# Key blocks transposed three products behind their own, and divisions put first, in a linear-attention and gated-MLP kernel

## The chip, the cores and the metric

The kernel runs on one core of a Trainium2 chip. The time is device microseconds of one execution: the median of three runs before the change is 2389.95 us (2389.79 to 2392.02). One execution was taken with the hardware profiler.

## The reference, cut to what matters

All arrays are fp32: x is 2048 x 1024, there are 32 heads of 32, and the MLP is 3584 wide. The output is the input plus attention times the activated MLP:

```python
xn = layernorm(x)
q, k, v = heads(xn @ wqkv)
phi = lambda t: where(t > 0, t + 1, exp(t)) + 1e-6
kv  = einsum("bhsd,bhse->bhde", phi(k), v)      # 32 x 32 per head
den = einsum("bhqd,bhd->bhq", phi(q), phi(k).sum over s) + 1e-6
s   = (phi(q) @ kv / den) @ wo
g   = silu((silu(xn @ w1) * (xn @ w3)) @ w2)
out = x + s * g
```

## The kernel before, in words

An fp32 product is made of three TensorE matmuls on high and low parts (`mm3`, L103 to L105; `split`, L95 and L96, makes the parts on ScalarE and VectorE). A 2 x 2 block product takes seven such products instead of eight (Strassen-Winograd); they are named by the weight operand, B11, T2, T3, T1, B21, T4, B22, and each is 12 matmuls of 128 x 512. `gemm` runs these seven, and between them VectorE forms the results from the banks a, b, c, d: c22 after T3 and T1, the first quadrant after B21, c21 after T4, c12 after B22 (L457 to L493). A name such as `ck1_0` is bank c of the key product of half 1, pair 0; `wk`, `wq`, `wg`, `wu` are weights of keys, queries, gates and ups.

The rows are taken in two halves of 1024 (h = 0, 1). In order of time the stages are: loading and normalising; keys, then queries of half 0; gates and ups of half 0; keys and queries of half 1, pair 0 of both product by product side by side, the other pairs one after another (757 to 927 us); the row products, which multiply keys and input rows (`g<-xy`, to 1107 us); gates and ups of half 1 (to 1690 us); the attention product (`cs`, `as` and so on with operands XA11s, XS3s, to 1835 us); the second MLP product.

A key block goes through `phi` (two ScalarE steps and a VectorE step, L499 to L501) into a tile `pk`, is then transposed by TensorE in four matmuls into a bank `trk` (`turn`, L507) and stored from there. `pk` has one of four buffers (`signed`), which it shares with the query blocks `pq` and others. `key_rows` puts each transposition into a list `later`. `gemm` calls `catch_up` after each product but the last: this does one transposition from `later` if there is one, and otherwise one step of the first entry of `jobs`, a list of generators that fill the gaps with other work. A job's step may be told (`issue_after`) to come behind a given instruction of its own engine.

In the gates of half 1 the job is `attention_work`: it multiplies g with the value weights (`kv<-gw`, L913), merges wo into it, and divides. `divide(m, k)` loads blocks of phi(q) (`pq_d`) and of the reciprocal denominators (`r_d`) with SyncE (L877, L879; SP in the trace), multiplies them and forms four sums on VectorE (L885, L730 to L734), and stores the operand blocks of the attention product (`qs_d`) through GpSimd's queue. There are 32 divisions, k = 0 to 3 for each m = 0 to 7. The gates and ups of half 1 call `catch_up` 28 x 6 = 168 times; `attention_work` has 152 steps. Its tiles come from four job buffers, which the jobs of the row products use too, and they are loaded some entries ahead of the steps. The attention product reads `qs_d` for m = 0 to 7 in that order.

The scheduler places instructions of an engine in the order that the code and its own estimates give; each engine then runs its instructions in that order.

Of the kernel before, what the change touches and what calls it, by code (L numbers as in the profile page):

```python
# [16 lines left out]
P = 128  # L17
# [5 lines left out]
def tile_linear_attention_times_swiglu(  # L23
# [12 lines left out]
    S, D = x.shape  # L36
    F = w1.shape[1]
    ND = D // P
# [3 lines left out]
    NCH = S // C  # L42
# [362 lines left out]
    def product(acc, B, A, start, stop=True):  # L405
        K = ND // 2
        for k in range(K):
            mm3(acc, (B[:, 0, k], B[:, 1, k]), (A[:, 0, k], A[:, 1, k]),
                start=start and k == 0, stop=stop and k == K - 1)

    later = []
    jobs = []

    def catch_up(*marks):

        if later:
            later.pop(0)()
        elif jobs:
            job, in_order = jobs[0]
            with ExitStack() as behind:  # L420
                for m in marks + (tuple(fetched) if in_order else ()):
                    behind.enter_context(tc.issue_after(m.ins))
                if next(job, None) is None:
                    jobs.pop(0)

    def gemm(B, A, use, early=False, paired=False, own=False):

        name = B.name

        B.upto("B11")
        u = (st.tile([P, C], F32, tag="own", bufs=1, name=f"u{name}") if own else
             pe.tile([P, C], F32, tag="u", name=f"u{name}"))
        ba = bank(f"a{name}")
        product(ba, B.upto("B11"), A["A11"], True)  # L440
        copied = nc.scalar.copy(out=u, in_=ba)
        if early:
            catch_up(copied)
            yield
            product(ba, B.upto("B21"), A["A12"], False)
            use(0, 0, ba)
            yield
            for _ in B.stages:
                pass
        else:  # L450
            next(stages, None)
            catch_up(copied)
            if paired:
                yield
        bb, bc, bd = (bank(f"{n}{name}") for n in "bcd")
        product(bb, B.upto("T2"), A["S2"], True)
        added = nc.vector.tensor_add(out=u, in0=bb, in1=u)  # L457
        next(stages, None)
        catch_up(copied, added)
        if paired:  # L460
            yield
        product(bc, B.upto("T3"), A["S3"], True)
        c22 = small(f"c22{name}")
        added = nc.vector.tensor_add(out=c22, in0=bc, in1=u)
        next(stages, None)
        catch_up(copied, added)
        if paired:
            yield
        product(bd, B.upto("T1"), A["S1"], True)
        added = nc.vector.tensor_add(out=c22, in0=bd, in1=c22)  # L470
        use(1, 1, c22)
        next(stages, None)
        catch_up(copied, added)
        if paired:
            yield
        if not early:
            product(ba, B.upto("B21"), A["A12"], False)
            use(0, 0, ba)
            next(stages, None)
            catch_up(copied, added)  # L480
        if paired:
            yield
        product(bc, B.upto("T4"), A["A22"], False)
        c21 = small(f"c21{name}")
        added = nc.vector.tensor_add(out=c21, in0=bc, in1=u)
        use(0, 1, c21)
        next(stages, None)
        catch_up(copied, added)
        if paired:
            yield  # L490
        product(bd, B.upto("B22"), A["S4"], False)
        c12 = small(f"c12{name}")
        nc.vector.tensor_add(out=c12, in0=bd, in1=u)  # L493
        use(1, 0, c12)
        next(stages, None)
# [17 lines left out]
    def key_rows(h, pair):  # L513

        rows = {}

        def use(n, c, src):
            j = 2 * pair + n
            pk = signed(f"pk{h}_{j}_{c}")
            z = st.tile([P, 1], F32, tag="z", name="z")  # L520
            phi(src, pk, z)
            nc.vector.scalar_tensor_tensor(zacc[:, j:j + 1], z, C * 1e-6, zacc[:, j:j + 1],
                                           op0=ALU.add, op1=ALU.add)
            later.append(lambda: turn(n, c, pk))

        def turn(n, c, pk):
            V = nc.vector
            p_ = turned(pk, f"k{h}_{pair}_{n}{c}")
            if (c, n) == (0, 0):
                y00 = small(f"y00_{h}_{pair}")  # L530
                nc.scalar.activation(y00, p_, AF.Identity, bias=eps)  # L531
                keep_keys(h, pair, "Y00", y00)
            elif (c, n) == (1, 1):
                rows["y01"] = job_tile([P, 2, C], f"y01_{h}_{pair}")
                nc.scalar.copy(out=rows["y01"][:, 1], in_=p_)
            elif (c, n) == (1, 0):
# [12 lines left out]

        return use  # L550

    def row_products():
# [39 lines left out]
        for at, s in enumerate(steps):  # L592
            i, h, t = s
            if at + 2 < len(steps):
                data[steps[at + 2]] = load(*steps[at + 2])
            if at + 1 < len(steps):
                split_[steps[at + 1]] = ready(*steps[at + 1])
            if at + 2 == len(steps):
                ops["g1_0_"].ask()
                stages = in_turn(groups[after_rows:])  # L600
            if at + 1 == len(steps):
                for _ in range(3):
                    next(stages)
            begins, ends = s[1:] == ks[0], s[1:] == ks[-1]
            onto = i in (1, 5)
            if begins and not onto:
                b = {m: bank(f"g{i}_{m}") for m in M}
            for e, (x_, y_) in enumerate(split_.pop(s)):
                for m in M:
                    c = slice(m * P, (m + 1) * P)  # L610
                    last = mm3(b[m], (x_[:, 0, c], x_[:, 1, c]), (y_[:, 0], y_[:, 1]),
                               begins and e == 0 and not onto, ends and e == 1)
                    if ends and e == 1:
                        row_sums(i, m, b[m], u, v)
                with tc.issue_after(last.ins):
                    catch_up()
                yield
            del data[s]

# [247 lines left out]
    def divide(m, k):  # L867
# [12 lines left out]
            return t  # L880

        def steps(t):
            for _ in range(3):
                yield True
            nc.vector.scalar_tensor_tensor(t[:, :2], t[:, :2], 1e-6, t[:, 2:], op0=ALU.add, op1=ALU.mult)  # L885
            for _ in four_sums(t[:, 0], t[:, 1], t[:, 2], t[:, 3], nc.vector):
                pass
            t = t.rearrange("p e (n s) -> p (e n) s", s=P)
            nc.gpsimd.dma_start(out=qs_d[m][:, 0, k], in_=t[:, 0])  # L889
            nc.gpsimd.dma_start(out=qs_d[m][:, 1:, k], in_=t[:, 2:])  # L890
            divided.add((m, k))
            yield True
# [66 lines left out]
        return [Job(lambda e=e: load(e), lambda t, e=e: steps(e, t)) for e in range(2)]  # L959


    LATE = S // (2 * P) - 2

    def late_work():
        yield from go_on([divide(m, k) for m in range(LATE, S // (2 * P)) for k in range(ND // 2)])

    H0, H1 = range(NCH // 2), range(NCH // 2, NCH)

    def all_denominators():
        yield from spread_z()  # L970
        yield from go_on([j for c in range(NCH) for j in denominators(c)])

    def attention_work():
        work = []
        for k in range(ND // 2):
            for e, j in enumerate(merge_wo(k)):
                work += key_values(k + e * (ND // 2)) + [j]
        work += [divide(NT * c + g, k) for c in H0 for g in range(NT) for k in range(ND // 2)]
        work += [divide(m, k) for m in range(NT * H1[0], LATE) for k in range(ND // 2)]
        yield from go_on(work, 3)  # L980


# [19 lines left out]
    stages = in_turn(groups[:after_rows])  # L1002
    for h in range(NH):
        half(h)
    jobs.append((late_work(), True))


    GT = 2 * P
# [261 lines left out]
    acc = []  # L1270
# [35 lines left out]
```

## Time and profile before

| | |
|---|---|
| median of three runs | 2389.95 us (2389.79 to 2392.02) |
| the profiled execution | 2391.7 us, span 2389.9 us |
| busy: TensorE, VectorE, ScalarE, GpSimd | 97%, 74%, 39%, 29% |
| mean granted clock of TensorE | 0.991 |
| DMA | 479.69 MB, 201 GB/s |

In the rows of the trace the first number is the start in microseconds, the second the duration, and square brackets hold how long the engine had stood before the instruction and what ended this. PE is TensorE, DVE VectorE, ACT ScalarE, POOL GpSimd; SP is the engine that issues most loads, SPq its queue, in which the issues follow one another. An engine that is busy for most of the span but stands at a few places can be sped up only at those places. The granted clock of a window is the share of full speed that TensorE had.

### The profile page before, as it was taken

To read this page: it belongs to the slowest core of one execution; us is meant where nothing else is said; L and a number is where in the kernel's file an instruction comes from. 1 tells how busy PE (TensorE), PEld (TensorE's weight loads), DVE (VectorE), ACT (ScalarE), POOL (GpSimd) and SP (SyncE) were. 2 spreads that over 40 slices of the span, in tenths; PEclk is the share of its full clock that TensorE was granted. 3 is DMA by queue.
4 is the path that set the end of the run, shared out by engine and by line. 5 is a ranking of instruction groups with operands and counts; after the bars stand their busy time and mean duration, and the time that the engine had idled before them with its cause. 6 is when DMAs were issued, how large, how long until landed. Compare 5 with 4: busy or idle time off the path is not lost.

```text
span 2389.9 us, 30981 instructions
## 1 busy us (share of the span) xinstructions
PE 2313.4 (97%) x10368; PEld 1895.4 (79%) x10368; DVE 1776.6 (74%) x2822; ACT 925.6 (39%) x1639; POOL 693.4 (29%) x852
## 2 busy tenths in 40 slices
PE   6899999999999899999999999999999999999998
PEld 5788888888887677777888888888777788888876
DVE  8887888887877565566777888887665676767698
ACT  5555343423332444433334232324323543343433
POOL 5210434386774111002243334242321000000033
PEclk9999999999999899999999999999999999999999
DMA  6545555666669435776666556564776665766588
GB/s 232 169 168 176 180 165 175 196 222 207 212 216 363 135 108 179 251 262 222 189 182 191 185 166 196 171 190 149 251 229 197 191 206 159 236 197 188 183 272 264
DMA packets 354015, 479.69 MB, mean 201 GB/s; under 512 B 24144, under 2 KB 262736, under 8 KB 353744
## 3 DMA queue, kind: packets, MB, share of 16 engines
q1 hardware_dynamic: 316608, 359.20, 47.4%
q0 software_dynamic: 37248, 118.52, 14.9%
q8 instruction: 81, 1.33, 0.2%
q14 instruction: 78, 0.64, 0.1%
HBM read 308.81 MB, written 172.49 MB: 201 GB/s over the span
## 4 chain that ended last, share of the span: by engine, by line
PE 42%; issue 9%; DMA 7%; DVE 5%; POOL 3%; ACT 1%; SPq 0%; POOLq 0%; DVEq 0%; ACTq 0%
PE g L103 2%; PE g L104 2%; PE g L105 2%; PE cB L103 1%; PE cB L104 1%; PE dB L104 1%; PE dB L103 1%; PE dB L105 1%; PE cB L105 1%; PE aB L103 1%; PE aB L104 1%; PE aB L105 1%; POOL h_d L751 1%; DMA xy<-y_d 1%; DMA qs_d<-qd 1%
## 5 line engine op out<-in xcount | busy, mean ns | idle before, releaser
L751 POOL DMA_DIRECT2D h_d<-sg x112 | 83.0, 741 | 284.4 <-DVE sg L747 184.3
L1073 POOL DMA_DIRECT2D u_d<-uB x32 | 17.4, 542 | 407.4 <-DVE uB L1056 392.8
L96 DVE TENSOR_TENSOR xy<-xy,xy 128x512 fp32r<-128x512 f32 x112 | 74.8, 704 | 67.5 <-ACT xy L95 67.5
L95 ACT CAST xy<-xy 128x512 fp32r<-128x512 f32 x112 | 65.1, 621 | 103.8 <-PE g L105 66.3
L104 PE MATMUL g<-xy,xy 128*128 128x512 f32 x224 | 87.6, 391 | 0.6 <-DVE xy L96 0.6
L105 PE MATMUL g<-xy,xy 128*128 128x512 f32 x224 | 87.2, 390 | 0.0
L103 PE MATMUL g<-xy,xy 128*128 128x512 f32 x224 | 81.6, 398 | 0.7 <-ACT xy L95 0.7
L511 POOL DMA_DIRECT2D y_d<-y x40 | 28.7, 719 | 138.3 <-ACT y L531 56.3
L1056 DVE TENSOR_TENSOR acc<-cB,acc 128x512 f32<-128x512 f32 x50 | 34.4, 689 | 41.5 <-PE cB L105 41.5
L1056 DVE TENSOR_TENSOR acc<-dB,acc 128x512 f32<-128x512 f32 x56 | 38.6, 689 | 31.6 <-PE dB L105 29.9
L889 POOL DMA_DIRECT2D qs_d<-qd x32 | 18.2, 568 | 150.1 <-DVE qd L885 137.9
L731 POOL TENSOR_TENSOR hs<-hs,sg 128x256 f32<-128x256 f32 x56 | 58.1, 1038 | 0.0
L733 POOL TENSOR_TENSOR hs<-sg 128x256 f32<-128x256 f32 x56 | 55.2, 986 | 0.0
L103 PEld LDWEIGHTS g<-xy,xy 128*128 128x128 f32 x224 | 41.6, 188 | 15.2 <-issue 4.5
L669 POOL DMA_DIRECT2D pq_d<-pq x32 | 17.5, 546 | 124.8 <-DVE pq L501 116.9
L730 POOL TENSOR_TENSOR hs<-sg,sg 128x256 f32<-128x256 f32 x56 | 50.1, 894 | 1.2
L104 PEld LDWEIGHTS g<-xy,xy 128*128 128x128 f32 x224 | 42.0, 188 | 10.2 <-DVE xy L96 1.0
L734 POOL TENSOR_TENSOR hs<-sg,hs 128x256 f32<-128x256 f32 x56 | 49.1, 877 | 1.8
L105 PEld LDWEIGHTS g<-xy,xy 128*128 128x128 f32 x224 | 42.1, 188 | 9.0
L759 POOL DMA_DIRECT2D h_d<-hs x60 | 46.1, 769 | 3.8 <-POOL hs L734 2.7
L766 POOL TENSOR_TENSOR w<-w 128x256 f32<-128x256 f32 x28 | 28.1, 1003 | 62.1 <-DMA w<-in_B_w 62.1
L1187 POOL DMA_DIRECT2D s_d<-s x32 | 17.5, 546 | 88.2 <-DVE s L1056 48.5
(5315 smaller groups left out, 8348.2 us busy)
## 6 DMA issues: line engine op xcount, KB each, us to landing
h_d<-hs POOLq DMA_DIRECT2D x60, 256.0 KB, 3.4
h_d<-sg POOLq DMA_DIRECT2D x56, 256.0 KB, 3.4
w<-in_B_w SPq DMA_DIRECT2D x56, 256.0 KB
wt_d<-w SPq DMA_DIRECT2D x28, 512.0 KB
xy<-x_d SPq DMA_DIRECT2D x28, 512.0 KB
xy<-y_d SPq DMA_DIRECT2D x28, 512.0 KB
h_d<-hs SPq DMA_DIRECT2D x52, 256.0 KB
qs_d<-qd POOLq DMA_DIRECT2D x32, 384.0 KB, 3.4
```

The lines of the kernel that those rows point to most:

```text
L95: nc.scalar.copy(out=hi, in_=src)
L96: return nc.vector.tensor_sub(out=lo, in0=src, in1=hi.bitcast(F32))
L103: nc.tensor.matmul(acc, lhsT=wh, rhs=ah, start=start, stop=False, skip_group_check=True)
L104: nc.tensor.matmul(acc, lhsT=wh, rhs=al, start=False, stop=False, skip_group_check=True)
L105: return nc.tensor.matmul(acc, lhsT=wl, rhs=ah, start=False, stop=stop, skip_group_check=True)
L730: e.tensor_add(out=s1, in0=a21, in1=a22)
L731: e.tensor_sub(out=s2, in0=s1, in1=a11)
L733: e.tensor_sub(out=s3, in0=a11, in1=a21)
L734: e.tensor_sub(out=s4, in0=a12, in1=s2)
L751: nc.gpsimd.dma_start(out=h_d[i][2 * h + c][:, 2 * n:4 * n + 2, k], in_=src)
L759: queue.dma_start(out=h_d[i][2 * h + c][:, 6 + 4 * e:10 + 4 * e, k], in_=o[e].rearrange("p (e s) -> p e s", s=P))
L1056: return V.tensor_add(out=c, in0=src, in1=c)
```

## The change

An entry of `later` carries a countdown of three, which every `catch_up` lowers; while it has not run out, `catch_up` goes on with the jobs. Each product of a gemm returns its last matmul, and the TensorE work of a `catch_up`, a transposition or a job's step, is put behind that matmul. `attention_work` starts with the eight divisions of m = 0 and 1, then has the key-value work, then the divisions of m = 2 to 7. A division takes three steps instead of four, so that the total stays 152. `late_work`, which held the eight divisions of m = 6 and 7 for the attention product, is gone.

```diff
     def product(acc, B, A, start, stop=True):
         for k in range(K):
-            mm3(acc, (B[:, 0, k], B[:, 1, k]), (A[:, 0, k], A[:, 1, k]),
-                start=start and k == 0, stop=stop and k == K - 1)
+            last = mm3(acc, (B[:, 0, k], B[:, 1, k]), (A[:, 0, k], A[:, 1, k]),
+                       start=start and k == 0, stop=stop and k == K - 1)
+        return last
     def catch_up(*marks):
-        if later:
-            later.pop(0)()
+        for e in later:
+            e[0] -= 1
+        if later and later[0][0] <= 0:
+            with ExitStack() as behind:
+                for m in marks[-1:]:
+                    behind.enter_context(tc.issue_after(m.ins))
+                later.pop(0)[1]()
         elif jobs:
...
-        product(bc, B.upto("T3"), A["S3"], True)
+        last = product(bc, B.upto("T3"), A["S3"], True)
         c22 = small(f"c22{name}")
         added = nc.vector.tensor_add(out=c22, in0=bc, in1=u)
         next(stages, None)
-        catch_up(copied, added)
+        catch_up(copied, added, last)
...
-            later.append(lambda: turn(n, c, pk))
+            later.append([3, lambda: turn(n, c, pk)])
...
-                with tc.issue_after(last.ins):
-                    catch_up()
+                catch_up(last)
...
         def steps(t):
-            for _ in range(3):
+            for _ in range(2):
                 yield True
...
-    LATE = S // (2 * P) - 2
-    def late_work():
-        yield from go_on([divide(m, k) for m in range(LATE, S // (2 * P)) for k in range(ND // 2)])
...
     def attention_work():
-        work = []
+        work = [divide(m, k) for m in range(2) for k in range(ND // 2)]
         for k in range(ND // 2):
             for e, j in enumerate(merge_wo(k)):
                 work += key_values(k + e * (ND // 2)) + [j]
-        work += [divide(NT * c + g, k) for c in H0 for g in range(NT) for k in range(ND // 2)]
-        work += [divide(m, k) for m in range(NT * H1[0], LATE) for k in range(ND // 2)]
+        work += [divide(m, k) for m in range(2, S // (2 * P)) for k in range(ND // 2)]
         yield from go_on(work, 3)
...
-    jobs.append((late_work(), True))
```

The first place is the end of pair 0 in half 1. TensorE before, where `dq` is the last product of the pair and `ak1_1` the first of the next:

```order
L105 MATMUL dq1_0__6513<-S4_1_6426,B22q1_0__6562 128x512
L507 MATMUL trk1_0_00_6643<-ident_63,pk1_0_0_6633 128x128 x4
L507 MATMUL trk1_0_01_6694<-ident_63,pk1_0_1_6685 128x128 x4
L103 MATMUL ak1_1__6776<-A11_1_6420,B11k1_1__6588 128x512
L104 MATMUL ak1_1__6776<-A11_1_6420,B11k1_1__6588 128x512
```

TensorE after:

```order
L105 MATMUL ak1_1__6765<-A11_1_6420,B11k1_1__6588 128x512
L513 MATMUL trk1_0_01_6784<-ident_63,pk1_0_1_6677 128x128 x4
L103 MATMUL bk1_1__6795<-S2_1_6421,T2k1_1__6633 128x512
L104 MATMUL bk1_1__6795<-S2_1_6421,T2k1_1__6633 128x512
L103 MATMUL ck1_1__6796<-S3_1_6422,T3k1_1__6611 128x512
```

The block `trk1_0_01` has moved behind the twelve matmuls of `ak1_1`; `trk1_0_00` has moved forward, behind the first two matmuls of `cq1_0` with T4. In pairs 1 to 3, where keys are followed by queries, `trk_00` and `trk_01` stood together ahead of the query product's `aq`; now `aq`, `bq` and `cq` stand ahead of, between and behind them: `aq`, `trk_00`, `bq`, `trk_01`, `cq`, `trk_10`, and between T4 and `trk_01` there are 38 matmuls.

VectorE at the same place before, from the next weights' sums (L346) to the key block `pk1_0_1`:

```order
L346 TENSOR_TENSOR wk1_1__6565<-wk1_1__6565 128x4x128 x2
L96 TENSOR_TENSOR T3k1_1__6618<-wk1_1__6565,T3k1_1__6618 128x512
L346 TENSOR_TENSOR wk1_1__6565<-wk1_1__6565 128x4x128
L485 TENSOR_TENSOR c21k1_0__6683<-ck1_0__6492,uk1_0__6455 128x512
L485 TENSOR_TENSOR c21q1_0__6717<-cq1_0__6512,uq1_0__6473 128x512
L493 TENSOR_TENSOR c12k1_0__6740<-dk1_0__6493,uk1_0__6455 128x512
L493 TENSOR_TENSOR c12q1_0__6763<-dq1_0__6513,uq1_0__6473 128x512
L96 TENSOR_TENSOR T2k1_1__6640<-wk1_1__6565,T2k1_1__6640 128x512
L96 TENSOR_TENSOR T1k1_1__6668<-wk1_1__6565,T1k1_1__6668 128x512
L96 TENSOR_TENSOR B21k1_1__6691<-wk1_1__6565,B21k1_1__6691 128x512
L346 TENSOR_TENSOR wk1_1__6565<-wk1_1__6565 128x4x128
L501 SCALAR_TENSOR_TENSOR pk1_0_1_6685,z_6686<-c21k1_0__6683,pk1_0_1_6685 128x512
```

VectorE after:

```order
L507 SCALAR_TENSOR_TENSOR pq1_0_0_6655<-aq1_0__6474,pq1_0_0_6655 128x512
L491 TENSOR_TENSOR c21k1_0__6675<-ck1_0__6492,uk1_0__6455 128x512
L507 SCALAR_TENSOR_TENSOR pk1_0_1_6677,z_6678<-c21k1_0__6675,pk1_0_1_6677 128x512
L491 TENSOR_TENSOR c21q1_0__6706<-cq1_0__6512,uq1_0__6473 128x512
L528 SCALAR_TENSOR_TENSOR zacc_77<-z_6678,zacc_77 128x1
L96 TENSOR_TENSOR B11k1_1__6588<-wk1_1__6565,B11k1_1__6588 128x512
L346 TENSOR_TENSOR wk1_1__6565<-wk1_1__6565 128x4x128
```

The key block now stands right behind its sum, and the next weights come behind both.

The second place is SP at the end of the row products, whose last operands are `xy6_12`. Before:

```order
L566 DMA xy6_10_8910<-x_d1_165 128x2x512
L564 DMA xy6_10_8910<-y_d1_167 128x2x512
L906 DMA gw0_0_9113<-in_A_wqkv 128x4x128
L566 DMA xy6_12_8964<-x_d1_165 128x2x512
L564 DMA xy6_12_8964<-y_d1_167 128x2x512
L326 DMA wg1_0__9019<-in_B_w1 128x8x256
```

After:

```order
L570 DMA xy6_10_8910<-y_d1_167 128x2x512
L882 DMA qd0_0_9113<-r_d0_136 128x1x256
L884 DMA qd0_0_9113<-pq_d0_0_79 128x256
L882 DMA qd0_0_9113<-r_d0_136 128x1x256
L884 DMA qd0_0_9113<-pq_d1_0_83 128x256
L882 DMA qd0_1_9118<-r_d0_136 128x1x256
L884 DMA qd0_1_9118<-pq_d0_0_79 128x256
L882 DMA qd0_1_9118<-r_d0_136 128x1x256
L572 DMA xy6_12_8964<-x_d1_165 128x2x512
L570 DMA xy6_12_8964<-y_d1_167 128x2x512
```

Seven loads of the first two divisions stand ahead of `xy6_12`, where one load of value weights stood.

The third place is SP at the start of the attention product. Before:

```order
L1145 DMA rA11q_2_13923<-qs_d2_130 128x512
L879 DMA qd6_0_13980<-pq_d0_3_82 128x256
L877 DMA qd6_0_13980<-r_d3_139 128x1x256
L1145 DMA rS2q_2_13928<-qs_d2_130 128x512
L879 DMA qd6_0_13980<-pq_d1_3_86 128x256
L877 DMA qd6_1_13985<-r_d3_139 128x1x256
L879 DMA qd6_1_13985<-pq_d0_3_82 128x256
L1145 DMA rS3q_2_13933<-qs_d2_130 128x512
L1145 DMA rS1q_2_13938<-qs_d2_130 128x512
```

After:

```order
L1141 DMA rA11q_2_14019<-qs_d2_130 128x512
L1141 DMA rS2q_2_14024<-qs_d2_130 128x512
L1141 DMA rS3q_2_14029<-qs_d2_130 128x512
L1141 DMA rS1q_2_14034<-qs_d2_130 128x512
L1141 DMA rA12q_2_14039<-qs_d2_130 128x512
```

The loads of the divisions of m = 6 are gone from between the operands.

More of the change, by code (lines that the diff above doesn't have):

```diff
@@ L439, in gemm @@
         ba = bank(f"a{name}")
-        product(ba, B.upto("B11"), A["A11"], True)
+        last = product(ba, B.upto("B11"), A["A11"], True)
         copied = nc.scalar.copy(out=u, in_=ba)
         if early:
-            catch_up(copied)
+            catch_up(copied, last)
             yield
@@ L451, in gemm @@
             next(stages, None)
-            catch_up(copied)
+            catch_up(copied, last)
             if paired:
@@ L455, in gemm @@
         bb, bc, bd = (bank(f"{n}{name}") for n in "bcd")
-        product(bb, B.upto("T2"), A["S2"], True)
+        last = product(bb, B.upto("T2"), A["S2"], True)
         added = nc.vector.tensor_add(out=u, in0=bb, in1=u)
         next(stages, None)
-        catch_up(copied, added)
+        catch_up(copied, added, last)
         if paired:
             yield
-        product(bc, B.upto("T3"), A["S3"], True)
+        last = product(bc, B.upto("T3"), A["S3"], True)
         c22 = small(f"c22{name}")
@@ L465, in gemm @@
         next(stages, None)
-        catch_up(copied, added)
+        catch_up(copied, added, last)
         if paired:
             yield
-        product(bd, B.upto("T1"), A["S1"], True)
+        last = product(bd, B.upto("T1"), A["S1"], True)
         added = nc.vector.tensor_add(out=c22, in0=bd, in1=c22)
@@ L472, in gemm @@
         next(stages, None)
-        catch_up(copied, added)
+        catch_up(copied, added, last)
         if paired:
@@ L476, in gemm @@
         if not early:
-            product(ba, B.upto("B21"), A["A12"], False)
+            last = product(ba, B.upto("B21"), A["A12"], False)
             use(0, 0, ba)
             next(stages, None)
-            catch_up(copied, added)
+            catch_up(copied, added, last)
         if paired:
             yield
-        product(bc, B.upto("T4"), A["A22"], False)
+        last = product(bc, B.upto("T4"), A["A22"], False)
         c21 = small(f"c21{name}")
@@ L487, in gemm @@
         next(stages, None)
-        catch_up(copied, added)
+        catch_up(copied, added, last)
         if paired:
@@ L959, in merge_wo @@
         return [Job(lambda e=e: load(e), lambda t, e=e: steps(e, t)) for e in range(2)]
-    LATE = S // (2 * P) - 2
-    def late_work():
-        yield from go_on([divide(m, k) for m in range(LATE, S // (2 * P)) for k in range(ND // 2)])
-    H0, H1 = range(NCH // 2), range(NCH // 2, NCH)
     def all_denominators():
```

## The prediction

> **What bounds the kernel.** I read the page's busy shares first, then the windows by stage, then what TensorE waited for, then the rows around the longest of those waits.
>
> ```profile
> span 2389.9 us, 30981 instructions
> PE 2313.4 (97%) x10368; PEld 1895.4 (79%) x10368; DVE 1776.6 (74%) x2822; ACT 925.6 (39%) x1639; POOL 693.4 (29%) x852
> ```
>
> TensorE is busy 97% of the span. Nothing in the change removes a matmul, so the gain can only come from the 3% in which TensorE stands, and from stretches in which it runs at a lower clock. The next windows (keys and queries of half 1; row products; gates of half 1 in two rows; attention product) show where those are. Columns: length, then busy time of PE, PEld, DVE, ACT, POOL, the granted clock, DMA share, GB/s.
>
> ```profile
> 757.00:927.00 170.00, 152.90 (x663) 124.67 (x663) 109.71 (x194) 79.81 (x137) 29.45 (x43) 0.94 0.46 157
> 1107.00:1120.00 13.00, 9.09 (x42) 6.70 (x41) 6.19 (x11) 2.87 (x5) 2.19 (x4) 1.00 0.60 188
> 1300.00:1500.00 200.00, 198.59 (x874) 163.38 (x873) 162.93 (x256) 63.92 (x109) 74.62 (x90) 1.00 0.58 181
> 1690.00:1835.00 145.00, 138.00 (x600) 112.71 (x599) 80.50 (x149) 38.30 (x67) 31.56 (x51) 0.99 0.70 219
> ```
>
> The keys and queries of half 1 lose 17.1 us to standing, and their mean clock is 0.94. The first 13 us of the gates lose 3.9, the attention product 7.0. The middle of the gates stands 1.4 us in 200, so there is nothing to win there, but VectorE is at 81%.
>
> ```profile
> PE trk L507 <- DVE pk L501: 16.9, 6, 5.7
> PE cs L103 <- DVE s L1063: 5.6, 2, 4.4
> PE tS L164 <- DVE pk L501: 2.9, 1, 2.9
> PE kv L913 <- DMA gw<-g_d: 2.8, 1, 2.8
> ```
>
> These are total, count, longest. The largest is the transposition of a key block (trk), which waits for VectorE to finish that block (pk).
>
> **Term 1: transposing later.** The first rows are the waits of pairs 0, 1 and 3 of half 1; pair 2 repeats pair 3, and the other two of the six are in half 0, with under 2 us between them.
>
> ```profile
> 800.30 1.12 PE L507 MATMUL trk<-ident,pk 128*128 128x128 f32 x4 [5.67 <-DVE pk L501]
> 827.03 1.08 PE L507 MATMUL trk<-ident,pk 128*128 128x128 f32 x4 [3.24 <-DVE pk L501]
> 917.84 0.91 PE L507 MATMUL trk<-ident,pk 128*128 128x128 f32 x4 [3.15 <-DVE pk L501]
> ```
>
> Is the block ready by the time at which it is now wanted? It comes from product T4, through a VectorE sum (c21k), two ScalarE steps and a VectorE step. The next rows give T4's last matmul, that sum and that step for pair 0 and then for pair 1, and two neighbouring starts of matmuls at full clock.
>
> ```profile
> 785.63 0.39 PE L105 MATMUL ck__6492<-A,T4k__6508 128*128 128x512 f32 x1
> 794.30 0.68 DVE L485 TENSOR_TENSOR c21k__6683<-ck__6492,uk__6455 128x512 f32<-128x512 f32 x1
> 799.55 0.69 DVE L501 SCALAR_TENSOR_TENSOR pk<-c21k__6683,pk 128x512 f32<-128x512 f32 x1 [0.37 <-ACT pk L500]
> 819.78 0.39 PE L105 MATMUL ck__6808<-A,T4k__6725 128*128 128x512 f32 x1
> 821.47 0.69 DVE L485 TENSOR_TENSOR c21k__6915<-ck__6808,uk__6775 128x512 f32<-128x512 f32 x1
> 826.19 0.69 DVE L501 SCALAR_TENSOR_TENSOR pk<-c21k__6915,pk 128x512 f32<-128x512 f32 x1 [0.73 <-ACT pk L500]
> 805.48 0.39 PE L104 MATMUL ak__6776<-A,B11k__6588 128*128 128x512 f32 x1
> 805.71 0.39 PE L105 MATMUL ak__6776<-A,B11k__6588 128*128 128x512 f32 x1
> ```
>
> A matmul starts every 0.23 us (0.2275 as the mean of long runs). Pair 1: T4 ends at 820.2, the block is ready at 826.9, 6.7 us later. In the new order 38 matmuls stand between T4 and this transposition, 8.6 us: covered, with 1.9 to spare; pairs 2 and 3 repeat pair 1. Pair 0 took 14.2 us, since VectorE had the next weights' sums and splits ahead of c21k and 5.3 us of other work behind it. The new order puts 48 matmuls and another transposition there (about 11.1 us), which alone would not cover 14.2; but it also puts c21k and the pk step directly one behind the other, ahead of the weights, so about 3 us remain (two VectorE steps of 0.7 and two ScalarE steps). All six waits should go: −16.9. What hides the transposition is the following products; if VectorE fell 2 us further behind in pairs 1 to 3, that cover would be gone and each late us would return as a wait. The matmuls of the transposition itself stay, four per block. The blocks live longer in their four buffers, which the queries share; in pair 0 the buffer of the first block is wanted two key blocks later, after its transposition.
>
> **Term 2: the clock after the waits.** Windows laid on the stretches in which the granted clock was half:
>
> ```profile
> 798.64:805.47 6.83, 5.17 (x14) 4.22 (x15) 6.43 (x15) 4.58 (x9) 2.39 (x4) 0.50 0.29 88
> 825.95:832.78 6.83, 5.75 (x16) 4.71 (x17) 2.80 (x8) 1.41 (x3) 1.44 (x2) 0.50 0.39 116
> 873.74:877.15 3.41, 3.41 (x10) 2.63 (x9) 1.27 (x5) 0.61 (x1) 1.45 (x2) 0.50 0.31 91
> 918.11:921.52 3.41, 3.41 (x11) 2.75 (x10) 1.17 (x5) 0.69 (x1) 1.46 (x2) 0.50 0.95 314
> 1713.41:1716.83 3.42, 2.84 (x7) 2.26 (x8) 2.33 (x4) 0.31 (x1) 0.54 (x2) 0.50 0.71 214
> ```
>
> Half of TensorE's busy time in each of the first four is lost: (5.17 + 5.75 + 3.41 + 3.41) / 2 = 8.9 us. If the waits go, this goes too: −8.9; if they only shrink to under 2 us, I expect the same, since the 2.80 us wait for the kv operand lies in a window at clock 1.00. The Trainium skill ("TensorE: Matmul & The Clock Gate", Part 1, The HAM clock gate) says that the clock halves after at least one idle window of about 3.4 us and returns after about as long of sustained work. By that alone the three gaps of about 3.2 us need not have cost any clock, and this term would be 2.6 instead of 8.9; the trace shows them at half clock, so the trace decides.
>
> **Term 3: divisions first.** At the start of the gates the key-value product stood 2.80 us for its operand; of the 3.9 us in the window above, 1.1 lie before that.
>
> ```profile
> 1090.97 0.74 SPq L564 DMA_DIRECT2D xy<-y_d  x1
> 1101.64 1.21 PE L103 MATMUL g<-xy,xy 128*128 128x512 f32 x4 [0.41 <-ACT xy L95]
> 1114.41 1.37 SPq L904 DMA_DIRECT2D gw<-g_d  x2
> 1117.35 1.16 PE L913 MATMUL kv<-gw 128*128 128x128 f32 x8 [2.80 <-DMA gw<-g_d]
> ```
>
> Eight divisions, with no TensorE work, now stand there, and the products come 24 steps later, when their operand is long written: −2.8. Against it: the loads of the first two divisions (r_d and pq_d, two each) enter SP's queue, seven of them ahead of the last row operands, whose issue at 1090.97 already ended in a wait of 0.41. Such a load takes SP about 0.53 us (a row of term 4), so up to 7 x 0.53 = 3.7 us late. Ends −3.9 (all that stands there) and 3.7 − 2.8 = +0.9; with a wait of the kv wait's size once more, for the weights behind them, +3.7. I take −1.5, since those loads can be issued while the operands still wait for a buffer.
>
> **Term 4: none left for the attention product.** The rows are the wait there, and back from it.
>
> ```profile
> 1713.99 0.79 PE L103 MATMUL cs<-wp,XA22s 128*128 128x512 f32 x1 [4.39 <-DVE s L1063]
> 1712.65 0.69 DVE L96 TENSOR_TENSOR XS3s<-rS3q,XS3s 128x512 fp32r<-128x512 f32 x1 [3.26 <-ACT XS3s L95]
> 1711.99 0.62 ACT L95 CAST XS3s<-rS3q 128x512 fp32r<-128x512 f32 x1 [3.33 <-DMA rS3q<-qs_d]
> 1704.51 0.38 SPq L1145 DMA_DIRECT2D rS3q<-qs_d  x1
> 1701.06 0.53 SPq L877 DMA_DIRECT2D qd<-r_d  x1
> ```
>
> TensorE waited for a sum that VectorE issues behind the split of XS3s, which waited for a load that SP issued among the divisions' loads. Five of these stand between rA11q and rS3q, about 0.5 us each, so the load goes out some 2.5 us earlier, and its transfer shares the DMA engines with less. The split still stands ahead of the sum in the new VectorE order, so the wait shrinks and need not vanish: 4.39 − 2.5 = 1.9, less what the lighter traffic gives. Below 3 us the half clock goes too (2.84 / 2 = 1.4). Ends: 0, and −4.39 − 1.4 − 1.2 (the second such wait, 5.6 − 4.39) = −7.0. I take −4.0: 2.5 + 1.4 and a little.
>
> **Term 5: where the divisions went.** A division's VectorE work, from all 32:
>
> ```profile
> L885 DVE SCALAR_TENSOR_TENSOR qd<-qd 128x512 f32<-128x512 f32 x32 | 21.8, 682 | 7.8 <-DMA qd<-pq_d 7.8
> L734 DVE TENSOR_TENSOR qd<-qd 128x128 f32<-128x128 f32 x32 | 15.6, 489 | 0.6
> L731 DVE TENSOR_TENSOR qd<-qd 128x128 f32<-128x128 f32 x32 | 9.6, 301 | 0.0
> 1410.34 3.85 DVE L346 TENSOR_TENSOR wu__11442<-wu__11442 128x512 f32<-128x512 f32 x2
> 790.87 1.40 DVE L346 TENSOR_TENSOR wk__6565<-wk__6565 128x512 f32<-128x512 f32 x2
> ```
>
> With three sums like L731 that is 0.68 + 0.49 + 3 x 0.30, about 2.0 us each. Steps of the gates last 583 / 168 = 3.5 us; one division per three steps instead of four raises VectorE's share from 2.0/13.9 to 2.0/10.4, by 5 points, from 81% to 86%. TensorE is still not waiting for it on the mean: 0, with −1.4 (all standing in that window) and +3 as ends; the upper end is one wait of the size of the kv wait. In half 0, VectorE and ScalarE keep their work and only the transpositions move: 0, from −1 to +2.9 (the tS wait above, the longest there on a key block).
>
> **Sum.** −16.9 − 8.9 − 1.5 − 4.0 = −31.3. The profiled execution took 2391.7 us (span 2389.9 and 1.8 around it), so 2360.4; the median of the runs, 2389.95, is 1.75 below it, so 2358.7, called 2359. All ends at their best: −16.9 − 8.9 − 3.9 − 7.0 − 1.4 − 1 = −39, 2351. All at their worst: −25.8 + 3.7 + 0 + 3 + 2.9 = −16.2, 2373.8.
>
> **Rivals.**
> - The waits change their place: VectorE's order differs, and TensorE waits for the next weights (T2, B21) instead of pk. For it: in pair 0 the weights' splits now come after c21k. Against: VectorE is busy 109.7 us of 170 there, so in 144 us still only 76%. If half of terms 1 and 2 comes back, −31.3 + 12.9 = −18.4, about 2372.
> - Slower: VectorE becomes the bound of the gates. In the rows above the same pair of sums took 3.85 us instead of 1.40 while GpSimd was at its own. With VectorE at 86%, a division could grow by 0.14 × 10.4 = 1.4 us, to 3.4, before TensorE waits; from there each us costs one per division. The 24 divisions behind the key-value work would have to take 3.4 + 31.3 / 24 = 4.7 us each to eat the gain, and 5.0 to show as slower: about 2397. Against it: the L734 rows, the worst hit of them, have a mean of 0.49. The Trainium skill ("GPSIMD Engine Reference", 1. Specifications) says that GpSimd shares SBUF interfaces with VectorE and contends with instructions that have two SBUF inputs, as these sums have; the rows agree in kind.
> - No change to speak of: the transpositions are placed later, yet TensorE's own queue stalls elsewhere by as much, at 2390. Only a chain longer than 11 us in all four pairs would do that; the 6.7 us of pair 1 speak against it.
>
> **Chances.** The forecast 0.66 (its own range 2351 to 2367); waits that change place 0.21 (2367 to 2385); no change 0.05; slower 0.08. A difference of 0.2% (4.8 us) is about what a measurement of this kernel can tell from none; faster than that: 0.66 + 0.21 = 0.87. The range that leaves out no more than 2 in 10 runs from 2350 to 2376: the best ends, and the worst ends with most of the first rival.
>
> **What would show it.** Term 1: no wait of trk for pk over 1 us in the windows of half 1, and that stage some 26 us shorter. Term 2: clock 1.00 there. Term 3: kv waits gone from the start of the gates, and the last g matmuls' wait not over 2 us. Term 4: the wait of cs for s around 2 us or less, no half clock. Term 5: VectorE at about 86% behind the key-value work, with TensorE standing under 5 us in the gates. I am wrong if the stage of half 1 keeps over 10 us of standing, or if TensorE waits for c22 or B operands in many gate products.

## The result, and the profile after

The changed kernel took 2364.74 us (median of 4 runs, 2364.22 to 2366.05); beside them the kernel before took 2390.98. The ratio is 0.9888, 95% interval 0.9871 to 0.9905: faster by 26.2 us, where 31 were forecast (2359; the range was 2350 to 2376). The profiled execution took 2364.7 us with a span of 2362.9, 27.0 shorter than before.

The head of the page after:

```profile
span 2362.9 us, 30966 instructions
PE 2306.2 (98%) x10368; PEld 1893.2 (80%) x10368; DVE 1775.7 (75%) x2822; ACT 924.5 (39%) x1639; POOL 697.2 (30%) x852
```

To compare stages, both traces were cut at the same matmuls: the first of half 1's keys, the first of the row products, of its gates, of the attention product, of the second MLP product. The windows before:

```profile
752.74:939.48 186.74, 169.64 (x737) 138.55 (x736) 119.69 (x208) 87.54 (x150) 32.61 (x48) 0.95 0.49 168
939.48:1107.25 167.77, 166.52 (x817) 127.29 (x816) 100.18 (x148) 67.27 (x117) 19.34 (x22) 1.00 0.75 248
1107.25:1120.00 12.75, 8.84 (x41) 6.51 (x40) 5.98 (x10) 2.87 (x5) 2.19 (x4) 1.00 0.59 184
1120.00:1693.97 573.97, 571.80 (x2575) 473.45 (x2573) 450.82 (x682) 202.77 (x352) 202.74 (x235) 1.00 0.59 183
1693.97:1836.81 142.84, 135.84 (x590) 110.94 (x589) 76.84 (x145) 37.44 (x65) 28.72 (x48) 0.99 0.69 216
```

and after:

```profile
751.70:917.64 165.94, 163.50 (x738) 134.18 (x737) 122.68 (x209) 88.01 (x148) 36.96 (x52) 0.98 0.56 190
917.64:1093.48 175.84, 168.72 (x817) 128.97 (x816) 99.93 (x147) 67.14 (x117) 19.25 (x22) 0.98 0.76 250
1093.48:1106.20 12.72, 11.69 (x52) 9.36 (x51) 11.82 (x21) 5.87 (x10) 2.71 (x5) 1.00 0.54 188
1106.20:1673.44 567.24, 567.15 (x2563) 471.09 (x2562) 451.02 (x713) 200.25 (x348) 217.47 (x250) 1.00 0.63 195
1673.44:1808.27 134.83, 133.60 (x589) 110.28 (x588) 65.63 (x103) 37.55 (x65) 18.04 (x33) 1.00 0.57 172
```

| stage | before | after | difference | forecast |
|---|---|---|---|---|
| up to the end of half 0's gates | 752.7 | 751.7 | −1.0 | −1.7 |
| keys and queries of half 1 | 186.7 | 165.9 | −20.8 | −24.1 |
| row products | 167.8 | 175.8 | +8.1 | with the gates −1.5 |
| gates of half 1 (both rows) | 586.7 | 580.0 | −6.8 | |
| attention product | 142.8 | 134.8 | −8.0 | −4.0 |
| the rest | 553.1 | 554.7 | +1.6 | 0 |

The row products hold the surprise: TensorE stands 7.1 us in them (175.84 − 168.72; 1.25 before), and the clock falls. What TensorE waited for, after (total, count, longest):

```profile
PE g L103 <- ACT xy L95: 7.1, 2, 6.9
PE tS L164 <- DVE pk L507: 2.9, 1, 2.9
PE bk__6491 L103 <- ACT T2k__6342 L95: 2.2, 1, 2.2
PE cg__2657 L103 <- DVE c22g__2689 L470: 2.1, 1, 2.1
PE cs L103 <- DVE s L1059: 1.2, 1, 1.2
```

Two waits near the start of the program are not listed, since they stand in both traces alike (tA, 11.4 us before and 11.2 after, and bk__735, 4.7 in both). No wait of a transposition (trk) is left, nor one of the key-value product. The longest wait is a new one, before the last row operands; the rows are that wait, the GpSimd step that it goes back to, and the SP issues that lead to it:

```profile
1085.66 2.07 PE L103 MATMUL g<-xy,xy 128*128 128x512 f32 x4 [6.87 <-ACT xy L95]
1082.63 2.33 POOL L583 TENSOR_TENSOR xy<-xy,yy 128x1024 f32<-128x1024 f32 x1 [8.67 <-DMA xy<-y_d]
1063.70 0.46 SPq L570 DMA_DIRECT2D xy<-y_d  x1
1064.26 0.66 SPq L882 DMA_DIRECT2D qd<-r_d  x1
...
1067.34 3.25 SPq L884 DMA_DIRECT2D qd<-pq_d  x1
1070.63 0.54 SPq L882 DMA_DIRECT2D qd<-r_d  x1
1071.29 1.08 SPq L572 DMA_DIRECT2D xy<-x_d  x1
1072.40 1.07 SPq L570 DMA_DIRECT2D xy<-y_d  x1
```

The same steps before:

```profile
1086.12 0.46 SPq L564 DMA_DIRECT2D xy<-y_d  x1
1086.64 0.49 SPq L906 DMA_DIRECT2D gw<-in_A_wqkv  x1
1090.57 0.36 SPq L566 DMA_DIRECT2D xy<-x_d  x1
1098.55 2.39 POOL L577 TENSOR_TENSOR xy<-xy,yy 128x1024 f32<-128x1024 f32 x1 [2.47 <-DMA xy<-y_d]
```

From one operand load to the last one SP took 8.70 us (1063.70 to 1072.40) where it took 4.85 (1086.12 to 1090.97): 3.85 later, in a queue that now held seven loads of the divisions. Before, SP issued one load of value weights in that time and then stood 3.4 us (1086.64 + 0.49 to 1090.57). After, the seven loads took 6.9 us (1064.26 to 1071.17), 3.25 of them one load alone, and used up that pause and more; why that one took so long the trace does not tell. From the issue of the last operand load to the GpSimd step it was 10.23 us (1072.40 to 1082.63) where it had been 7.58 (1090.97 to 1098.55): 2.65 longer, with the divisions' transfers under way beside it. 3.85 + 2.65 = 6.5, and the wait grew by 6.87 − 0.41 = 6.5. Behind it TensorE ran at half clock:

```profile
1085.30:1088.80 3.50, 3.14 (x7) 2.48 (x8) 1.90 (x3) 1.35 (x3) 0.00 (x0) 0.50 0.55 167
1088.80:1092.20 3.40, 3.40 (x13) 2.72 (x12) 1.29 (x2) 0.62 (x1) 0.00 (x0) 0.76 0.93 255
```

3.14 x 0.50 + 3.40 x 0.24 = 2.4 us are lost by it.

### The profile page after: what moved, and what is told of

Same layout as the page of the kernel before. It is cut to its first block, busy times and chain, and to the rows that moved or that the text cites. A ratio compares the mean times of both kernels' runs of the same rounds, so it can differ in the third digit from the quotient of the medians.

```text
span 2362.9 us, 30966 instructions
## 1 busy us (share of the span) xinstructions
PE 2306.2 (98%) x10368; PEld 1893.2 (80%) x10368; DVE 1775.7 (75%) x2822; ACT 924.5 (39%) x1639; POOL 697.2 (30%) x852
## 4 chain that ended last, share of the span: by engine, by line
PE 74%; DMA 5%; DVE 5%; issue 2%; ACT 1%; SPq 1%; POOL 0%; DVEq 0%; POOLq 0%; ACTq 0%
PE g L103 2%; PE g L104 2%; PE g L105 2%; PE cB L103 1%; PE cB L104 1%; PE cB L105 1%; PE dB L103 1%; PE dB L104 1%; PE dB L105 1%; PE aB L105 1%; PE aB L103 1%; PE aB L104 1%; DMA rA12B<-h_d 1%; PE bB L105 1%; PE bB L103 1%
```

## The experiments

Theory: the terms act at different places and add up; the delay of the transpositions, not their place in line, removes the waits; the loads that the first divisions put on SP and on the DMA engines make the last row operands late; the divisions in the attention product were what delayed it. Rivals stand with each run.

**Each half of the change alone.** `turns` has the change's `later`, `catch_up` and `gemm`, with the divisions as before:

```diff
-            for _ in range(2):
+            for _ in range(3):
...
-        work = [divide(m, k) for m in range(2) for k in range(ND // 2)]
+        work = []
...
-        work += [divide(m, k) for m in range(2, S // (2 * P)) for k in range(ND // 2)]
+        work += [divide(NT * c + g, k) for c in H0 for g in range(NT) for k in range(ND // 2)]
+        work += [divide(m, k) for m in range(NT * H1[0], LATE) for k in range(ND // 2)]
...
+    jobs.append((late_work(), True))
```

`divs` has these lines the other way round on the kernel before, whose transpositions stay.

> Only the transpositions three products later, in line on TensorE; the divisions as before (after the key-value work, eight in the attention product, four steps each). Theory (the terms add up): keys and queries of half 1 about 166 us as with the whole change (187 before), the row products stay at 168 and the attention product at 143, so about 2391 - 22 = 2369. Rival (the new wait in the row products comes from the jobs' TensorE work being put behind each product's last matmul): the row products grow to 176 here too, so about 2377.

> Only the divisions moved (eight first, none in the attention product, three steps each); the transpositions as before. Theory: row products 176 us with a wait of about 7 us before the last operands, gates of half 1 some 6 us shorter, attention product 135, keys and queries of half 1 still 187: about 2391 - 6 = 2385. Rival (the six waits were partly caused by late work of the same kind elsewhere, so that the parts do not add up): keys and queries of half 1 differ from 187 by over 3 us.

> The changed kernel once more, on the same chip as the three others: 2364 to 2366, with the wait of about 7 us in the row products again if it belongs to the order and not to one execution.

On one chip, beside 2392.41 of the kernel before: `turns` 2367.25 (ratio 0.9894, 0.9867 to 0.9922), `divs` 2384.69 (0.9976, 0.9962 to 0.9991), the whole change again 2365.11 (0.9886, 0.9863 to 0.9909), with the wait in the row products at 6.4 us. The gains 25.2 and 7.7 make 32.9 against 27.3 of the whole, a difference no larger than the intervals allow; about 3 us of it lie in the keys and queries of half 1, which take 165.9 us in both traces of the whole change and 163.0 in `turns`. The stages separate cleanly. Cut at the same matmuls, keys and queries of half 1 are 163.0 us in `turns` and 185.9 in `divs`; row products 166.9 and 176.0; gates 586.2 and 580.0; attention product 142.3 and 134.7. So the new wait belongs to the divisions, not to putting the jobs' TensorE work behind each product. The waits in `divs`:

```profile
PE trk L507 <- DVE pk L501: 16.9, 6, 5.7
PE g L103 <- ACT xy L95: 7.3, 2, 6.8
```

Here stand the old waits and the new one together.

**Delay or place in line.** In `c1` and `c2` the countdown is 1 or 2; in `nomark` it is three, and the transpositions are not put behind the product's last matmul. These are `c1` and `nomark`:

```diff
-            later.append([3, lambda: turn(n, c, pk)])
+            later.append([1, lambda: turn(n, c, pk)])
```

```diff
             with ExitStack() as behind:
-                for m in marks[-1:]:
-                    behind.enter_context(tc.issue_after(m.ins))
                 later.pop(0)[1]()
```

> The countdown is 1: each transposition is put in line right behind the product at which its block was made, as far as the order allows. Theory: the four waits of half 1 are back, at 3 to 6 us with half clock behind them, so about 2365 + 21 = 2386. Rival (putting the transpositions in line was what helped, not their delay): 2365 to 2370.

> The whole change, but the transpositions are not told to come behind the product's last matmul. Theory (the delay does it, the mark nothing): within 2 us of the changed kernel, 2363 to 2367, no wait of a transposition. Rival (without the mark they slip forward into their product and wait again): waits of trk for pk, 2370 or more.

> The countdown is 2 instead of 3: each transposition one product earlier. Theory (the cover counts): pairs 1 to 3 have 26 matmuls, 5.9 us, between T4 and the transposition of that block, against a chain of 6.7, so waits of about 1 us or less each in half 1, no or little half clock: 2365 to 2370. Rival (any later place will do): 2365 as with three.

`c1` took 2388.86 us (0.9976, 0.9966 to 0.9986), the same ratio as `divs`, and its waits of transpositions are those of the kernel before to the digit:

```profile
PE trk L513 <- DVE pk L507: 16.9, 6, 5.7
```

`nomark` took 2364.65 (0.9883, 0.9866 to 0.9899), with no trk wait. The delay does it; the mark adds nothing that can be measured.

The delay acts in two ways that no run takes apart: the transposition comes later, and the block is ready sooner, since VectorE's order changes with it. From T4's end to the finished block it is 14.2 us in pair 0 and 6.7 in each of the others, before and in `c1`; in the changed kernel it is 3.3, 4.1, 2.8 and 2.8. The transposition now starts 9.0 us behind T4's end in pairs 1 to 3, which would cover 6.7 even with the old order, and 11.2 us behind it in pair 0, which would not cover 14.2.

`c2` took 2360.28 (0.9856, 0.9839 to 0.9872): not slower than three, as I expected, but faster by 4.8 us than the whole change again, by the medians. My expectation took 6.7 us for the chain from T4 to the block, as before; but VectorE's order has changed. Pair 1 in `c2`:

```profile
805.97 0.39 PE L105 MATMUL ck__6796<-A,T4k__6714 128*128 128x512 f32 x1
808.68 0.69 DVE L507 SCALAR_TENSOR_TENSOR pk<-c21k__6907,pk 128x512 f32<-128x512 f32 x1
```

The block is ready 3.0 us after T4's end (808.68 + 0.69 − 805.97 − 0.39), and its transposition starts 6.2 us after that end. So the gain over three lies elsewhere. By stages the trace of `c2` is 2.8 us shorter than that of the changed kernel up to the end of half 0's gates, 5 us shorter in the keys and queries of half 1, and 3.0 longer in the second MLP product, where the edit does nothing. In the first two stages the 2.1 us wait of cg is gone and the 2.2 us wait of bk for T2k has shrunk to 0.7. Both have half clock behind them in the changed kernel, which these windows of it show:

```profile
299.00:306.00 7.00, 4.88 (x16) 3.57 (x15) 5.98 (x9) 2.34 (x5) 1.88 (x3) 0.76 0.64 195
757.00:764.50 7.50, 5.06 (x12) 3.31 (x11) 7.34 (x10) 4.76 (x10) 4.58 (x6) 0.66 1.05 400
```

Ahead of each late step VectorE work ran long while GpSimd was busy (ahead of bk, 3.21 us for a sum that takes 0.7 elsewhere). That one product less of countdown moves the jobs of half 0 by a step and so takes them apart is argued, not shown.

**The divisions first.** `order1` puts their first loads behind the last row operands in SP's queue, `order2` behind the load of the first gate weights, which stand behind those. `kvfirst` has the key-value work first and all 32 divisions behind it.

```diff
+                self.asked = nc.sync.dma_start(out=self.raw, in_=columns(self.w, self.c0, 2 * P))
+                fetched[:] = [self.asked]
...
-        jobs.append((attention_work(), False) if h else (next_work(), True))
+        jobs.append((behind_weights(attention_work()), False) if h else (next_work(), True))
...
+    def behind_weights(job):
+        with tc.issue_after(ops["g1_0_"].asked.ins):
+            first = next(job)
+        yield first
+        yield from job
```

This is `order2` (`asked` is the load of those weights); `order1` marks the last load of `row_products` in its place, and `kvfirst` is this:

```diff
-        work = [divide(m, k) for m in range(2) for k in range(ND // 2)]
+        work = []
...
-        work += [divide(m, k) for m in range(2, S // (2 * P)) for k in range(ND // 2)]
+        work += [divide(m, k) for m in range(S // (2 * P)) for k in range(ND // 2)]
```

> The whole change, but the first loads of the divisions are put behind the last row operands in SP's queue. Theory (the place in the queue makes the row operands late): the 6.9 us wait before the last row operands falls to about 0.4 us and its half clock goes, the row products are back at 168, so about 2365 - 8 = 2357. Rival (the extra traffic of the divisions' loads on the DMA engines makes them late, wherever they stand nearby): a wait of 3 us or more is left, about 2361 or more.

> The whole change, but the key-value work comes first and all 32 divisions behind it. Theory: the row products are back at 168 us; the wait of the key-value product for its operand is back at about 2.8 us and the two before it; so about 2365 - 8 + 3 = 2360. Rival (the divisions first win more than they cost, by their even spread): slower than the changed kernel, 2366 or more.

> The whole change, but the first loads of the divisions are put behind the load of the first gate weights in SP's queue, so behind the last row operands too. Theory (those loads take time from whatever large load they share the DMA engines with): neither the last row operands nor the first gate weights are waited for over 1 us; row products and the first 13 us of the gates are some 4 us shorter than with the loads behind the row operands alone, about 2358. Rival (TensorE then waits for the second weights or for VectorE, which stands for the late operand of a division): 2361 to 2363.

`order1` took 2361.79 (0.987, 0.9847 to 0.9893), 3.3 us less than the changed kernel on the same chip and not 8. The wait before the row operands is gone, and another stands a little later:

```profile
PE ag__9096 L103 <- ACT B11g__9047 L95: 4.0, 1, 4.0
```

The first gate weights are late. They were issued behind nine of the divisions' loads, and what followed was slow too; the rows are the issue and the first use in `order1`:

```profile
1074.68 0.77 SPq L326 DMA_DIRECT2D wg__9019<-in_B_w  x1
1085.31 0.62 ACT L95 CAST B11g__9047<-wg__9019 128x512 fp32r<-128x512 f32 x1 [8.04 <-DMA wg__9019<-in_B_w]
```

and in `order2`:

```profile
1072.49 0.37 SPq L326 DMA_DIRECT2D wg__9019<-in_B_w  x1
1080.41 0.62 ACT L95 CAST B11g__9047<-wg__9019 128x512 fp32r<-128x512 f32 x1 [2.54 <-DMA wg__9019<-in_B_w]
```

It is 10.6 us from issue to use in `order1` and 7.9 in `order2`, where the load was issued 2.2 earlier; in the kernel before, with none of the divisions' loads about, it was 5.2 (1097.42 to 1102.64). So both theory and rival held in part: the place in the queue made the row operands late, and the divisions' loads also slow a large load that stands beside them. The Trainium skill ("DMA: Bandwidth & Descriptors", Issuing engines are not separate DMA queues) says that DMAs run on the same 16 engines and interleave, whichever engine started them. The 2.65 us above and the 10.6, 7.9 and 5.2 here agree as to the sharing; the loads in question are all SP's, so that it holds across issuers is not shown.

`order2` took 2351.97 (0.9831, 0.9814 to 0.9849); its row products take 167.3 us, and there is no wait of either kind over 1 us. By the traces its row products are 3.6 us shorter than in `order1` and its gates 2.0, about as expected. That its median lies 6 below the expectation, and 13 below the changed kernel, is not explained: the row products, beside the two traces of the changed kernel, give 6.5 to 8.6 of it.

`kvfirst` took 2363.07 (0.9869, 0.985 to 0.9888): row products back at 167.1, the kv wait back at 2.7 us, 3 us above my 2360. Its gates, with all 32 divisions in them, take 585.0 us, no more than the 586.2 of `turns` with 24: VectorE does not become their bound.

**None left for the attention product.** `late` gives it the eight divisions of m = 6 and 7 back.

```diff
+    LATE = S // (2 * P) - 2
+
+    def late_work():
+        yield from go_on([divide(m, k) for m in range(LATE, S // (2 * P)) for k in range(ND // 2)])
...
-        work += [divide(m, k) for m in range(2, S // (2 * P)) for k in range(ND // 2)]
+        work += [divide(m, k) for m in range(2, LATE) for k in range(ND // 2)]
...
+    jobs.append((late_work(), True))
```

> The whole change, but the eight divisions of m = 6 and 7 are given back to the attention product. Theory: the attention product returns from 135 to about 143 us with a wait of cs for s of 3 us or more, the gates stay: about 2372. Rival (the gates gain from having fewer divisions what the attention product loses): 2365.

It took 2369.02 us (0.9895, 0.9878 to 0.9912), 3 less than expected. By its interval the total cannot be told from the changed kernel's; the stages can. The attention product is 140.5 us against 134.8, the gates 580.3 against 580.0, and the wait is back:

```profile
PE cs L103 <- DVE s L1065: 4.0, 1, 4.0
```

The gates gain nothing from the eight divisions that leave them.

**Together.** `best` is `order2` with countdown 2, `kvc2` is `kvfirst` with countdown 2.

> The two that helped, together: countdown 2, and the first loads of the divisions behind the first gate weights. Theory (they act at different places and add up): 2360 - 7 = 2353. Rival (the gain of countdown 2 is one of phase, which any other edit can undo): 2357 or more.

> Countdown 2, and the key-value work first, all 32 divisions behind it. Theory: the gain of countdown 2 (5 us) comes on top of 2363: 2358. Rival (its gain is one of phase): 2361 or more.

`best` took 2346.22 us (0.9806, 0.9788 to 0.9824), 1.9% less than the kernel before and a further 0.8 points beyond the change. `kvc2` took 2354.28 (0.9843, 0.9824 to 0.9862). They lie 7 and 4 us below the expectations. In all three surroundings countdown 2 gained (4.8, 5.8 and 8.8 us by medians; the first across two chips and the last across two rounds of runs, between which the kernel before differed by 1.5 us or less), so it is not a matter of one lucky phase that the next edit undoes. In `best` and `kvc2`, as in `c2`, the wait of cg is gone and that of bk for T2k is 1.1 us or less, where `order2` and `kvfirst` have 1.8 to 2.1 and 1.5 to 2.0. The head of `best`:

```profile
span 2344.4 us, 30961 instructions
PE 2299.0 (98%) x10368; PEld 1888.9 (81%) x10368; DVE 1772.1 (76%) x2822; ACT 924.5 (39%) x1639; POOL 694.1 (30%) x852
```

## Why the prediction was right, and where not

**Term 1** (−16.9) held in full: no trk wait is left. The recorded count of 38 matmuls in pairs 1 to 3 is 36 and two transpositions, which changes nothing. The chain of 6.7 us there was taken from the old order; in the new one it is 2.8 to 4.1, so the cover was wider than forecast. The working held in pair 0 too: "about 3 us remain", and it was 3.3:

```profile
787.76 0.39 PE L105 MATMUL ck__6492<-A,T4k__6508 128*128 128x512 f32 x1
790.78 0.69 DVE L507 SCALAR_TENSOR_TENSOR pk<-c21k__6675,pk 128x512 f32<-128x512 f32 x1 [1.90 <-ACT pk L506]
```

**Term 2** (−8.9) held behind those four waits, but not for the whole stage: the clock there is 0.98, not 1.00. The step "if they only shrink to under 2 us, I expect the same, since the 2.80 us wait for the kv operand lies in a window at clock 1.00" was drawn from one case and did not hold: waits of 2.12 and 2.25 us do have half clock behind them. The wait of bk for T2k, which the upper end for half 0 and its boundary only touched, is 2.2 us, where two such waits had made 1.8, but now there is half clock behind it, which takes most of the 3.3 us that are missing in that stage; in `turns`, where it is 1.7 us, the stage has clock 1.00 and takes 163.0. Its length alone does not decide this: in `nomark` it is 1.7 us too, with the same 2.4 us of standing in the stage, and the clock is 0.99. The last section says what does.

**Term 3** was the step that failed. It was −1.5 with an upper end of +3.7, "since those loads can be issued while the operands still wait for a buffer". The place was named, and a pause of 3.4 us that could cover the loads was there. What failed is the price of the loads: seven times 0.53 makes 3.7 us, which that pause would nearly have covered, but they took 6.9, and the two operand loads behind them were issued more slowly as well (1.08 and 1.07 us against 0.36 and 0.74). That SP's delay of 3.85 agrees with the 3.7 of the upper end, which reckoned with no cover, is luck. Two more costs were not in the sum: the transfer that the divisions' loads slow by 2.65 us, and 2.4 us of half clock behind the longer wait. The row products grew by 8.1 us. The other side held: kv's wait and the 3.9 us in the first 13 us of the gates shrank to 1.0 (12.72 − 11.69). Together the term is about +5 in place of −1.5, beyond its upper end, and `order2` shows that it could have been negative: with the row products at 167.3 it loses nothing.

**Term 4** (−4.0) was too small: −8.0, beyond its end of −7.0. Standing fell from 7.0 to 1.2 us and the half clock went. The wait of cs for s, expected to shrink to about 1.9, is 1.2. The step that took 2.5 us for SP's issues looked in the wrong place: without the divisions' loads rS3q goes out 3.73 us behind rA11q (1677.99 to 1681.72) where it was 4.30, only 0.6 sooner. Most of the gain is in the landing: from that issue to the split it is 3.8 us (to 1685.55) where it was 7.5, with 172 GB/s in that stage for 216. `late`, where the wait is 4.0 again, shows that the divisions were its cause.

**Term 5** (0) was near for its reason: VectorE did not become the bound, as `kvfirst` and `late` show. It is busy 84% of 1400 to 1600 us, behind the key-value work, where 86% were forecast, and TensorE does not stand there at all. TensorE stands 0.1 us in 567 behind the start of the gates, where it stood 2.2. The 6.8 us less in the gates as a whole are 5.0 of standing and 1.8 that the rows don't place; without the part that belongs to term 3 they are 3.9, more than the end of −1.4.

**The rivals.** The waits changed their place in a way, but not to the weights of the same pairs: to the end of the row products, and by the other half of the change. VectorE as the bound fell, and so did "no change". In the profiled execution the sum came out 4.3 us off: +7 in term 3, +3 behind the T2k wait and +1.6 in the rest were partly paid by 4 more in term 4 and 4 more in the gates. Terms 3, 4 and 5 fell outside their own ends, and the errors went against each other; that the total came so near is in part luck.

## What to carry to other kernels

If an in-order engine waits at one place for a chain on two others, put two products of other work between rather than a mark on its place, and read from the new order of the feeding engine how long that chain now is. Before a job is moved to an earlier time, list what its loads stand ahead of in the queue, and count the transfer that they slow as well as the issue that they delay: here the row products alone took 6.5 to 8.6 us more or less by where the first loads of the same divisions stood. A wait that is made longer or shorter by some microseconds can carry a clock loss behind it, and that belongs into the price on both sides.

## What the runs showed of the hardware that was not expected

The clock halved after waits much shorter than those seen before: 2.12 us (at 302 us) and 2.25 us (at 759 us) were each followed by matmuls that start 0.43 us apart instead of 0.23, while 2.80 us (before, at 1117) was not. A length alone does not tell. The rows are the first of these waits in the changed kernel:

```profile
302.06 0.79 PE L103 MATMUL cg__2657<-A,T4g__2570 128*128 128x512 f32 x1 [2.12 <-DVE c22g__2689 L470]
302.66 0.63 PE L104 MATMUL cg__2657<-A,T4g__2570 128*128 128x512 f32 x1
303.08 0.63 PE L105 MATMUL cg__2657<-A,T4g__2570 128*128 128x512 f32 x1
303.51 0.63 PE L103 MATMUL cg__2657<-A,T4g__2570 128*128 128x512 f32 x1
```

What does tell is where the wait falls. Within a trace the stretches of half clock start whole steps of 3.413 us apart. Before, they start at 798.64, 825.95, 873.74, 918.11 and 1713.41 us: 8, 14, 13 and 233 steps. In the changed kernel, starts at 301.96, 759.35 and 1083.61 are 134 and 95 steps apart. Carried on, these starts divide the whole trace, and what counts is how long TensorE stands within one step. Of the 2.12 and 2.25 us, 2.01 and 2.05 fall into the step that ends where the half clock starts; the 2.80 us are cut into 1.53 and 1.27 by a step's end at 1116.08, 58 steps behind 918.11. From 100 us after the start to 20 us before the end, in all 14 traces, each of the 40 steps at full clock with 1.8 us of standing or more was followed by half clock, 8 of the 34 with 1.3 to 1.8, and none with less. So a wait of 2 to 3 us may carry no clock loss at all, or 1.7 us (half of a step) and more, by where it falls.
